# Thresholded attention with an FFN behind it: P left unscaled, 1/sum multiplied in at x, and some half tiles masked by GpSimd

## The chip, the core and the metric

The kernel runs on one core of a Trainium2 chip. The metric is the device time of one execution in microseconds (us). TensorE is called PE in the profile, VectorE DVE, ScalarE ACT, GpSimd POOL and SyncE SP.

## The reference

```
scores = q @ k^T / sqrt(64)                     # 8 batches, 8 heads, 576 rows, 64 columns
thresh = max(scores, -1) - tau                  # tau = 0.02
scores = where(scores >= thresh, scores, -1e9)
attn   = exp(scores - max(scores))
attn   = attn / (sum(attn, -1) + 1e-9)
x      = attn @ v                               # laid out as 4608 tokens x 512
h      = max(x @ w1, x @ w2, x @ w3)            # 512 x 768 each
out    = h @ w_out                              # 768 x 512
```

Of each row of 576 scores only those within tau of the row's maximum count. The rest gives zero.

## The kernel before

**Tiling.** A batch is cut into two quads of four heads. The four heads of a quad are two couples: r is 0 or 1, and i is the head within the couple. A quad has nine chunks, each of 128 rows of queries (chunk 4 holds the last 64 rows of two heads). A chunk has two half tiles, r = 0 and r = 1, each 128 x 576 scores. That makes 8 x 2 x 9 x 2 = 288 half tiles. q and k are loaded as rows and transposed on TensorE (`transposed`), and `swapped` copies qt to qs with the partition halves exchanged, so that two matmuls of 64 rows can run side by side.

**One half tile.** `scores` (line 324) writes sc, a PSUM bank. `maximum` (line 364) reads it on VectorE, writes z to SBUF and the row's maximum to nm. Then there are four kinds, given half tile by half tile by the digits of `MASKED`:

- kind 0: `threshold` makes th on VectorE, `exponents` runs a Prelu on ScalarE from z with the slope 2^-100 on one side, so that what is kept comes out tiny and what is masked does not, and `numerators` runs an Exp on ScalarE with scale -2^100 and its row sum
- kind 2 ("direct"): the same, with the Prelu reading the PSUM bank itself, which stays occupied until then
- kinds 1 and 3 (3 is direct): one Exp on ScalarE, then a `scalar_tensor_tensor` on VectorE that zeroes what lies below exp(-tau) and sums

All of them leave z in place. When both half tiles of a chunk are summed, `reciprocals` (line 396) makes rs on VectorE and `normalized` (line 400) makes P = z x rs in bf16, two instructions on GpSimd. `turned` (line 409) transposes P from SBUF to SBUF by a DMA on SP's queue, into ptq.

**From P to the output.** `product` (line 415) multiplies v by ptq into a PSUM tile o when all nine chunks of a quad are there. It is evacuated to xt in bf16: r = 0 by VectorE (`on_vector`), r = 1 by ScalarE (`on_scalar`). When both quads of a batch are in xt, `ffn` computes the three products ph with w1, w2 and w3 for six blocks of 128 (18 pieces, `hid`), takes their maximum (hm on ScalarE, then twice on VectorE, into hT) and multiplies with w_out (`outp`, `ninth`, `ninths_of_two`), evacuates po to ob and stores it. The last batch is split into two parts of its rows, chunks 0 and 1 and chunks 2 to 4 (`SPLIT`), which makes 18 parts of quads in all.

**Pools.** PSUM has four slots of two banks, chosen by the digit behind S, T, O, F and N in `ORDER`. z has nine buffers and, after the first 72, also the two of stage, through which the weights are loaded. P has six buffers.

**Order.** Every engine issues in program order, and SP's and ScalarE's DMAs are in that order too (`_Ordered` adds the ordering; all instructions issue at line 93, so that the profile shows L93 for nearly all of them). The order is the string `ORDER`, one letter an action. The letters that matter here: S scores, m maximum, s threshold, e the first pass, n the Exp of kinds 0 and 2, k the mask of kinds 1 and 3, r reciprocals, p one half of the normalization, t the DMA transpose, O product, x and w the evacuation of x by ScalarE and VectorE, F an FFN piece (18 hidden ones a part, then the outputs), v and h the evacuations of ph, u that of po, l loads, g and z loads and casts of weights, q and y the copies of q and v on GpSimd.

Of the kernel before, what the change touches and what calls it, by code (L numbers as in the profile page):

```python
# [11 lines left out]
F32 = mybir.dt.float32  # L12
# [3 lines left out]
OP = AluOpType  # L16
# [5 lines left out]
FLAT = 2.0 ** -100  # L22

MASKED = """
232222322322222222021032222202332122123122200200111000000000100000000011
000010111020011000101000000001100001001000010011111100000000100100000000
110010030111000100010000000001010100001110001011010100110000000000000000
100101101011000000120000001010000000110011100000001110001000010011111021
# [6 lines left out]
MORE_Z = 72  # L35
# [5 lines left out]
llllllglllT0laclT1laclzllqqS0qqS1meS2mS3lmlT0enlkS1ylmlT2eamelrnpS3leqlmnyS1qcapS0emtnrcS3pmnT2qmepgrelS1qya  # L41
gS0pmelT2mqnS3tcpemqS2nlkT1eytaS0rmnT1kpermS3yS2enczrmS1qT0enmepnqtS3nprmaymgpeS0lptS2mppT0mtpS1enencnqsS3re
rmtpS0mS1penmS3lqnsS2mtperpekzllmT0tmpenkT1pgS3eearnS0petmnqrS2meqlnpS3lmnplsS2cetpremS1pS0nmplermtzeS3mnS2p
mtnpmS3rkpS1leektS0emnrpmemptS1eekS2pO3mktS0rennmpermT2pnS1wptemS3prkyO0tmeakS2pgS1enxlnrmS0lpesS2mezT3mS1np
mgntspcS2eqrseT3mtpeS0srmapS1mnT2ptS3mnqO0ceqmeO1prswnptnkS3pxS0meF1meS2zBresmT0qghF3klpF2nkBtaS1sveS0pemF3B
nyrrsmyBepT1svS0hpcT2nS3zmaS1erpgsF2mntpsBmnS3yvF1etssT0myeBprS2cnpS3mnS0ympelF2epF3lmBnzslssvS0htBrqmeS2vpn
S1gF0sepmF3teqBmF2erssvpBtnBkphF0eS1vtS3znmF2nrBmqteS1rpvBnS3pmlnF0pmgeS1qsBsrhmS3pevS2npS1mF0npsO3ermpesmO2
zewepgsskBxtT3nF1vS2nklBarS0mlphS3mtepF2sS1rmnyBmetF3pvT0eBpcnS2tzT1nvS0asmzS3temS2qeS1meF0trkpmS3lenpBmnlys
reklpF1umerpskS3upBeoketmS0uS2umpS3tesmS1qeT0myO2nqlrsnlprcO3etqsmepwS0xptS1mnF3psnmS2BlerskpS1thF0meF3pmeBF
2ktnBveBsrS1nvpS0hmyF3emF2npBrssT0eprtvBaF1kS3nqvBeF0myhyS2kyleF3mBelBvnpS2snsS0vptemS1pnF3rmpT2tnBmpeF0scS1  # L50
htBrnmpF3erT2rpvlBasS1pstvnS2pmeF0pS3emtBqnmT2S1hcqS3empF2eS0rsqmtS1epsmBeF3pmnF0stsvBeBknF2klhF1BvelS0nrvpB
emT3pS2arvS0ptnS3mpnO1smtesrkpeF2swnlrpmeT0S1qtescS3epBmnpmnT0trskS3paS1umS0ulqmeS3lmyS1nopS2smelS0rmeS3psmn
O1ypersmqO2etkpemO0lewqxlknpS3tS1keF2momS3lexF0ktT1enkBercpnsBpumN1ertkphkF3jS0rursS1empBnmF2ptS0vpS1smeF3yt
BsnsmBpnvS0pT1hmF2atT3srepS0cF1eprBsmeqF3vnByBynvplS2nsS0plmhS1mteS2mF0nF3mteS1rrspBnmS2pelvBlepF1smT0leqBvl
aS2rkhF3oqnsS0mtS1epmBeqsF2ssmtS0epvBeyF1mnF3vpBesrS0ktphBermS1npT2svO0nytmpncT3eS1wF2nrmS0aBrsmnqF3vnT1pS0c
eBptsF2mhpS1eS3pmteS0qmBeO1spmnkteF3rvnpT0BsskapS2xvS0erS1qmtnS3pmnF2mqlespmeS1rtkBepresmT3puS1cuS0ptmnS3pS2
meyS1lrekpF0tnsmempO3lekteskO2nrsmpeBkpxrnwS1uptS3muS2pnmF0yoeS1mF3lesymBtnS2srkpS1hmBeF0spveF2ertBmpT3nrsvS
1paBlmpnS0tS3qhmF1epsmS2leBymF3tevF0nBknlS1rsvpS2esmqnBF3srmhpS1epS0tmeF2pssBrempBtesvS0ynF1mT3lnpBvF0lhsrcS
2tnT1mBnF3valS2nrBsqmeF0pvS1epS2meBptsmS3eqF1hmT2peBcS3tnskT2O0arkplnmO2lerpvewptS3xkpS1nF2meF0sstreBsmpS3nv
pBnmS1tS2hmT3eF0rmpnF1cBpnBrevptT3S2apvS0qmtS3S1enmqF2esrsqmiepmleS0soykeS1plBnmemtS3ukS0uT1snrlO2cpekynO1me  # L60
# [44 lines left out]
def kernel(  # L105
# [44 lines left out]
    def weight_loads():  # L150


        def piece(dst, src):
            my = {}

            def load():
                my["t"] = stage.tile([128, 4 * 256], F32, name="stage")
                sync.dma_start(out=my["t"].rearrange("p (k f) -> p k f", k=src.shape[1]), in_=src)
# [241 lines left out]
    def normalized(c):  # L400
        c["P"] = P = pp.tile([128, W], BF16, name="P")
        for n in range(2):
            pool.tensor_scalar(out=P[:, n * S:(n + 1) * S], in0=c["z", n],
                                    scalar1=c["rs"][:, n:n + 1], scalar2=1.0, op0=OP.mult, op1=OP.mult)
            if n:
                line["t"].append(c)
# [423 lines left out]
```

## Time and profile before

| | us |
|---|---|
| median of 3 runs | 447.64 |
| lowest and highest of them | 447.23 and 447.99 |
| span of the profiled execution, first to last instruction | 444.8 |
| median less that span | 2.8 |

The profiled execution is told by its span. A run's time also holds what lies ahead of the first instruction and behind the last, 2.8 us if the profiled execution was like the median. In the profile's groups a row gives line, engine, operation, output<-inputs, shapes and count, then the busy time and the mean duration of one in ns, then the engine's idle time ahead of them and what ended it. Durations of neighbours overlap, so the step from one start to the next is shorter than a duration. Rows of stretches of time give each engine's busy time, the granted clock of TensorE, the mean busy share of the DMA engines (it can be over 1, as packets overlap) and GB/s.

### The profile page before, as it was taken

The numbers are of one execution on the slowest core, as the hardware profiler recorded it, in microseconds if no ns is written. First come the engines' busy times: TensorE is split into PE (matmuls) and PEld (weight loads), VectorE is DVE, ScalarE is ACT, GpSimd is POOL, SyncE is SP. The second block draws the span as 40 slices with busy tenths as digits, with TensorE's granted clock in tenths as the row PEclk, the third lists the DMA queues.
The fourth block names the chain that finished last, engine by engine and source line by source line (L and its number), as shares of the span: only waits on it lengthen the run. The fifth ranks groups of instructions, "written<-read, shape, count | busy, mean of one in ns | idle before, by whom it ended". The sixth has DMA issues, their size and how long they took to land.

```text
span 444.8 us, 14254 instructions
## 1 busy us (share of the span) xinstructions
PE 422.4 (95%) x5188; PEld 320.2 (72%) x5190; DVE 392.8 (88%) x1228; ACT 403.0 (91%) x836; POOL 311.9 (70%) x420
## 2 busy tenths in 40 slices
PE   7767789999999999999999999999999999999996
PEld 6334347787788767787788777788688886787873
DVE  3887999999999999999999999998999998899642
ACT  3999999999999999999999999899999999987632
POOL 2799989997878687696785877676676685457400
PEclk8998999999999999999999999999999999999999
DMA  7999999999999999699899999989999977487633
GB/s 188 275 293 199 291 169 269 235 243 262 229 180 194 212 222 292 125 256 167 143 234 189 230 198 203 209 168 210 208 206 194 244 151 105 83 179 136 145 116 108
DMA packets 213959, 88.50 MB, mean 199 GB/s; under 512 B 189184, under 2 KB 202240, under 8 KB 213888
## 3 DMA queue, kind: packets, MB, share of 16 engines
q1 hardware_dynamic: 213360, 86.96, 95.9%
q8 instruction: 41, 0.67, 0.6%
q10 hardware_dynamic: 528, 0.62, 0.5%
q14 instruction: 30, 0.25, 0.2%
HBM read 35.65 MB, written 9.44 MB: 101 GB/s over the span
## 4 chain that ended last, share of the span: by engine, by line
PE 86%; ACT 5%; DVE 4%; issue 2%; DMA 1%; SPq 0%; DVEq 0%; ACTq 0%
PE ph L93 32%; PE sc L93 32%; PE po L93 10%; PE o L93 9%; ACT z L93 5%; PE tp L93 3%; DVE z L93 3%; DMA qm<-in_q_dram 1%; ACT qt L93 1%; SPq L93 0%; DVE xt L93 0%; DVE hm L93 0%; DVE stage L93 0%; DVE rs L93 0%; ACT ob L93 0%
## 5 line engine op out<-in xcount | busy, mean ns | idle before, releaser
L93 POOL TENSOR_SCALAR P<-z,rs 128x576 bf16<-128x576 f32 x250 | 200.6, 814 | 63.3 <-DVE rs L93 28.1
L93 DVE TENSOR_SCALAR_CACHE_REDUCE z<-sc 128x576 f32<-128x576 f32 x250 | 183.7, 750 | 14.8 <-PE sc L93 10.1
L93 PE MATMUL sc<-kt,qs 64*128 64x256 f32 (+2 forms) x640 | 182.6, 423 | 5.7 <-DVE z L93 2.3
L93 PE MATMUL sc<-kt,qt 64*128 64x320 f32 (+2 forms) x640 | 182.4, 433 | 5.2 <-ACT z L93 3.3
L93 PE MATMUL ph<-xt,w 64*128 64x288 bf16 (+2 forms) x2160 | 170.8, 283 | 0.1
L93 PEld LDWEIGHTS <-w 64*128 64x128 bf16 (+1 forms) x2160 | 130.1, 94 | 28.6 <-issue 4.3
L93 ACT ACTIVATE z<-z 128x576 f32<-128x576 f32 x174 | 117.6, 679 | 0.1
L93 PEld LDWEIGHTS sc<-kt,qs 64*128 64x128 f32 (+1 forms) x640 | 92.4, 180 | 25.7 <-DVE z L93 5.7
L93 ACT ACTIVATE z<-z,th 128x576 f32<-128x576 f32 x143 | 106.2, 769 | 5.0 <-DVE th L93 4.2
L93 PEld LDWEIGHTS sc<-kt,qt 64*128 64x128 f32 (+1 forms) x640 | 91.9, 179 | 19.7 <-ACT z L93 5.9
L93 DVE SCALAR_TENSOR_TENSOR z<-z 128x576 f32<-128x576 f32 x76 | 62.2, 830 | 0.5 <-ACT z L93 0.5
L93 PE MATMUL po<-wo,hT 64*128 64x512 bf16 (+3 forms) x454 | 53.5, 354 | 0.3
L93 POOL COPY qs<-qt 64x640 f32<-64x640 f32 (+3 forms) x66 | 43.0, 652 | 10.8 <-ACT qt L93 7.2
L93 ACT ACTIVATE z<-z,nm 128x576 f32<-128x576 f32 x68 | 50.6, 767 | 0.0
L93 DVE TENSOR_TENSOR hm<-ph,hm 128x576 bf16<-128x576 f32 (+2 forms) x54 | 37.0, 686 | 9.2 <-PE ph L93 8.9
L93 ACT ACTIVATE hm<-ph 128x576 bf16<-128x576 f32 (+2 forms) x54 | 31.8, 589 | 13.4 <-PE ph L93 12.8
L93 POOL TENSOR_SCALAR P<-stage,rs 128x576 bf16<-128x576 f32 x38 | 30.4, 804 | 19.3 <-ACT z L93 5.4
L93 PEld LDWEIGHTS <-hT 64*128 64x128 bf16 (+2 forms) x456 | 30.0, 95 | 16.5 <-issue 2.3
L93 DVE TENSOR_TENSOR hT<-ph,hm 128x576 bf16<-128x576 f32 (+2 forms) x54 | 37.0, 686 | 4.0 <-PE ph L93 2.3
L93 PE MATMUL o<-ptq,vb 128*64 128x64 bf16 (+2 forms) x544 | 39.0, 281 | 0.0
L93 ACT ACTIVATION_READ_ACCUMULATOR z<-z 128x1 f32 x174 | 34.3, 197 | 0.0
L93 PEld LDWEIGHTS <-vb 128*64 128x64 bf16 x544 | 23.3, 111 | 12.8 <-issue 4.9
(45 smaller groups left out, 431.6 us busy)
## 6 DMA issues: line engine op xcount, KB each, us to landing
vm<-in_v_dram SPq DMA_DIRECT2D x32, 256.0 KB, 4.8
qm<-in_q_dram SPq DMA_DIRECT2D x15, 512.0 KB, 5.0
km<-in_k_dram SPq DMA_DIRECT2D x15, 512.0 KB, 5.3
out_dram<-ob SPq DMA_DIRECT2D x14, 512.0 KB, 4.0
stage<-in_moe_w_dram SPq DMA_DIRECT2D x9, 512.0 KB, 5.2
ptq<-P SPq DMA_TRANSPOSE x144, 4.0
vr<-in_v_dram SPq DMA_DIRECT2D x16, 128.0 KB, 3.4
stage<-in_moe_w_out_dram SPq DMA_DIRECT2D x3, 512.0 KB, 4.9
```

Of the source, the lines that this page charges most:

```text
L93: ins = fn(*a, **kw)
```

## The change

P is left unscaled. `numerators` writes P itself, in bf16, each half into its place, and gives the row sum to a column of one tile per quad, `sm` (`sum_of`). `normalized` and `reciprocals` per chunk are gone, so that the transpose follows the second half's numerators.

For each part of a quad the new `reciprocals` takes 1/sum of all chunks on VectorE and transposes the 128 x 32 tile in blocks of 32 x 32. `scale_rows` (letter D) stores the result to DRAM, on SP's queue, and `scale_tile` (letter R) reads it back by two DMAs, each spread to 64 partitions, into R, a buffer of stage. The product's evacuation is one `tensor_tensor` on VectorE for both r = 0 and r = 1: xt = o x R.

39 half tiles become kind 4. `threshold` makes th = nm + tau, `set_apart` (letter b) runs two instructions on GpSimd, a `tensor_scalar` that writes 2^100 where z > th and 0 elsewhere, and a `tensor_tensor` that adds this to z. Then one Exp on ScalarE with its sum (letter X) writes P. The counts by kind (0, 1, 2, 3, 4) are 169, 78, 33, 8, 0 before and 141, 75, 22, 11, 39 after.

The half tiles of z no longer use stage, ob9 takes buffers of z, small tiles have 8 buffers and not 6, and `ORDER` and `MASKED` are new throughout.

```diff
 FLAT = 2.0 ** -100
+FAR = 2.0 ** 100
 MASKED = """
...
-    def half_of_z():
-        n = next(halves_of_z)
-        if n >= MORE_Z and (n - MORE_Z) % (ZBUFS + 2) >= ZBUFS:
-            return stage.tile([128, 4 * 256], F32, name="stage")[:, :S]
-        return zz.tile([128, S], F32, name="z")
+    def by_pool(c, r):
+        return by_mask[2 * number[c["g"], c["idx"]] + r] == "4"
...
     def threshold(c, r):
         th = c["th", r] = small.tile([128, 1], F32, name="th", bufs=5)
-        vector.tensor_scalar(out=th, in0=c["nm", r], scalar1=-1.0, scalar2=tau, op0=OP.mult, op1=OP.subtract)
+        if by_pool(c, r):
+            vector.tensor_scalar(out=th, in0=c["nm", r], scalar1=tau, scalar2=None, op0=OP.add)
+        else:
+            vector.tensor_scalar(out=th, in0=c["nm", r], scalar1=-1.0, scalar2=tau, op0=OP.mult, op1=OP.subtract)
+    def set_apart(c, r):
+        z, m = c["z", r], half_of_p(c, r)
+        pool.tensor_scalar(out=m, in0=z, scalar1=c["th", r], scalar2=FAR, op0=OP.is_gt, op1=OP.mult)
+        pool.tensor_tensor(out=z, in0=z, in1=m, op=OP.add)
...
     def numerators(c, r):
-        z, acc = c["z", r], c["sm"][:, r:r + 1]
-        if masked(c["g"], c["idx"], r):
-            vector.scalar_tensor_tensor(out=z, in0=z, scalar=thr, in1=z,
+        z, p, acc = c["z", r], half_of_p(c, r), sum_of(c, r)
+        if by_pool(c, r):
+            scalar.activation(out=p, in_=z, func=AF.Exp, bias=c["nm", r], scale=-1.0, accum_out=acc)
+        elif masked(c["g"], c["idx"], r):
+            vector.scalar_tensor_tensor(out=p, in0=z, scalar=thr, in1=z,
                                         op0=OP.is_ge, op1=OP.mult, accum_out=acc)
         else:
-            scalar.activation(out=z, in_=z, func=AF.Exp, scale=-1.0 / FLAT, accum_out=acc)
-    def reciprocals(c):
-        c["rs"] = small.tile([128, 2], F32, name="rs")
-        vector.reciprocal(c["rs"], c["sm"])
-    def normalized(c):
-        c["P"] = P = pp.tile([128, W], BF16, name="P")
-        for n in range(2):
-            pool.tensor_scalar(out=P[:, n * S:(n + 1) * S], in0=c["z", n],
-                                    scalar1=c["rs"][:, n:n + 1], scalar2=1.0, op0=OP.mult, op1=OP.mult)
+            scalar.activation(out=p, in_=z, func=AF.Exp, scale=-1.0 / FLAT, accum_out=acc)
...
+    def reciprocals(g, part, n):
+        L, t = Ls[g], turns[n % 2]
...
+            vector.reciprocal(new[:, :, f:f + 9], sums[:, :, f:f + 9])
...
+            vector.reciprocal(new[to, :, at:at + 1], sums[of, :, was:was + 1])
+        vector.transpose(t[:, 1, :], t[:, 0, :])
+    def scale_rows(g, part):
+        s["rows"] = rows.tile([32, 128], F32, name="rows")
+        sync.dma_start(out=s["rows"].rearrange("j (b t) -> b j t", b=4), in_=s["t"][:, 1, :])
+    def scale_tile(g, part):
+        s["R"] = stage.tile([128, W], F32, name="stage").rearrange("p (r n) -> p r n", r=2)[:, :, 0:n]
...
+        for i in range(2):
+            sync.dma_start(out=s["R"][64 * i:64 * i + 64],
+                           in_=src[i, :, o:o + n].unsqueeze(0).to_broadcast([64, 2, n]))
...
-        def on_vector():
-            vector.tensor_copy(out=dst[:, lo:hi], in_=ps[:, base:base + hi - lo])
-        def on_scalar():
-            scalar.activation(out=dst[:, lo:hi], in_=ps[:, base:base + hi - lo], func=AF.Copy)
+        def done():
+            vector.tensor_tensor(out=dst[:, lo:hi], in0=ps[:, base:base + hi - lo],
+                                 in1=scales[2 * L["b"] + L["qd"], part]["R"][:, r, :], op=OP.mult)
```

185 lines of the change are left out of this document (112 added, 73 removed).

## The prediction

> **What bounds the kernel now.** I read the page's head first, then busy time in three stretches, then the groups by shape, then the waits of the first stretch.
>
> ```profile
> span 444.8 us, 14254 instructions
> PE 422.4 (95%) x5188; PEld 320.2 (72%) x5190; DVE 392.8 (88%) x1228; ACT 403.0 (91%) x836; POOL 311.9 (70%) x420
> L93 PE MATMUL ph<-xt,w x2160: 272/283/299, 73.1 to 435.5; 64*128 64x288 bf16 x184, 128*128 128x320 bf16 x7, 128*128 128x256 bf16 x6
> core 0: us, PE busy (x) PEld busy (x) DVE busy (x) ACT busy (x) POOL busy (x), PEclk, DMA share, GB/s
> 0.00:73.00 73.00, 56.29 (x502) 33.94 (x503) 58.19 (x178) 63.96 (x138) 56.99 (x81) 0.93 1.07 239
> 73.00:412.00 339.00, 337.74 (x4407) 265.23 (x4405) 320.55 (x1021) 326.61 (x672) 250.10 (x334) 1.00 1.00 198
> 412.00:444.80 32.80, 28.38 (x284) 21.03 (x282) 14.11 (x33) 12.43 (x29) 4.77 (x7) 0.99 0.44 125
> ```
>
> The first FFN matmul (ph) starts at 73.1 us. Before it TensorE has only scores and products to do and stands idle for 73.00 - 56.29 = 16.7 us. ScalarE is the busiest there (63.96), VectorE has 58.19 and GpSimd 56.99. So the opening runs at the pace of **ScalarE**. From 73 to 412 us TensorE is busy 337.74 of 339.00 us: the middle is **TensorE's**, with ScalarE at 96% and VectorE at 95% close behind. The last 33 us are one chain of TensorE and evacuations.
>
> ```profile
> 126.33 2.94 PE ph L93 x48
> 195.04 1.96 PE ph L93 x32
> PEld sc L93 <- ACT z L93: 10.0, 19, 1.0
> PEld sc L93 <- DVE z L93: 5.9, 7, 1.8
> ```
>
> In the chain of waits an FFN matmul costs 2.94 / 48 = 0.061 us, and 1.96 / 32 = 0.061 us elsewhere: where TensorE has work it goes at one rate, and nothing a vector engine gives back makes it faster. The two waits are those of the opening (0 to 73 us): score matmuls that stand until ScalarE (10.0 us) or VectorE (5.9 us) has freed a PSUM bank. So a gain must come from the opening, from the 1.3 us of idle TensorE in the middle, or from the end.
>
> **The change part by part.** I take the steps of the engines from rows that stand back to back, since one instruction's end overlaps the next one's start.
>
> ```profile
> 99.31 0.68 ACT L93 ACTIVATE z<-z 128x576 f32<-128x576 f32 x1
> 99.89 0.20 ACT L93 ACTIVATION_READ_ACCUMULATOR z<-z 128x1 f32 x1
> 99.98 1.44 ACT L93 ACTIVATE z<-z,th 128x576 f32<-128x576 f32 x2
> 100.22 0.76 DVE L93 TENSOR_SCALAR_CACHE_REDUCE z<-sc 128x576 f32<-128x576 f32 x1
> 100.91 0.15 DVE L93 TENSOR_SCALAR th<-nm 128x1 f32<-128x1 f32 x1
> 100.97 0.75 DVE L93 TENSOR_SCALAR_CACHE_REDUCE z<-sc 128x576 f32<-128x576 f32 x1
> L93 ACT ACTIVATE z<-sc,nm 128x576 f32<-128x576 f32 x39 | 28.3, 746 | 2.9 <-DVE z L93 2.9
> L93 DVE SCALAR_TENSOR_TENSOR z<-z 128x576 f32<-128x576 f32 x76 | 62.2, 830 | 0.5 <-ACT z L93 0.5
> L93 DVE RECIPROCAL rs<-sm 128x2 f32<-128x2 f32 x144 | 22.0, 157 | 2.0 <-ACT z L93 1.4 <-ACT stage L93 0.2
> L93 DVE CAST xt<-o 128x576 bf16<-128x576 f32 x14 | 10.5, 749 | 0.5 <-PE o L93 0.5
> L93 ACT ACTIVATE xt<-o 128x576 bf16<-128x576 f32 x14 | 9.0, 640 | 0.2
> L93 DVE TENSOR_TENSOR hm<-ph,hm 128x576 bf16<-128x576 f32 x42 | 31.5, 751 | 0.8 <-PE ph L93 0.6
> L93 POOL TENSOR_SCALAR P<-z,rs 128x576 bf16<-128x576 f32 x250 | 200.6, 814 | 63.3 <-DVE rs L93 28.1 <-ACT z L93 11.6 <-DVE th L93 7.4
> 0.00:73.00 73.00, 36.58 (x46) 0.93 1.07 239
> ```
>
> Steps: ScalarE's Exp with its sum 99.98 - 99.31 = 0.67 us; a Prelu from z 1.44 - 0.77 = 0.67; a Prelu straight from PSUM about 0.64 (its 746 ns less the same overlap of 0.1). VectorE's maximum 0.69, its threshold 0.06, a masking multiply 0.75 (830 ns less 0.08). The last row counts GpSimd's instructions on P alone (its one number of busy time): 36.58 us in the opening.
>
> *ScalarE in the opening.* The order issues, ahead of its first FFN piece, 50 first passes and 37 Exps before (37 of those passes direct from PSUM), and 34 first passes, 23 Exps and 12 masked Exps after, 10 of the passes direct. Before: 37 x 0.64 + 13 x 0.67 + 37 x 0.67 = 57.2. After: 10 x 0.64 + 24 x 0.67 + 35 x 0.67 = 45.9. The two x evacuations that leave ScalarE there are 2 x 0.53 = 1.1 more. Together 12.4 us less: 64.0 becomes 51.6.
>
> *VectorE in the opening.* One more maximum (+0.7), 31 thresholds for 8 (+1.4), 11 masking multiplies for 12 (-0.75), 4 x evacuations for 2 (+1.3), 23 small reciprocals gone (0.08 each in step, -1.8), and for two units the new reciprocals with a 32x32 transpose. That transpose has no row; between the small reciprocal (0.16) and the 749 ns cast I take 0.2, the small one, as it streams 32 columns. That is 0.36 a unit, +0.7. Sum +1.6: 58.2 becomes 59.8. **VectorE takes over as the busiest.** The multiply by R reads a second f32 operand from SBUF; its bounds are the 751 ns of hm and the masking multiply's 830; I take 751.
>
> *GpSimd.* Its 36.6 us on P go. 12 half tiles come, each a tensor_scalar of one input (0.81) and an add of two inputs, which no row shows: between 0.81 and twice that, 1.6, for two inputs read one after the other. I take 1.6, so 12 x 2.4 = 28.8 and 57.0 becomes 49.2, below VectorE at either end. The Trainium skill (GPSIMD Engine Reference, § 4.1 Engine selection and § 3.1) says that two-input elementwise work belongs on VectorE, GpSimd being about half as fast at 2.6 cycles an element; by that an estimate of 576 x 2.6 / 1.2 GHz = 1.25 us for the add, and the sum stays.
>
> So the opening's busiest engine falls from 64.0 to 59.8 us: **-4.2**. Half tiles that hold a PSUM bank until ScalarE has read it fall from 37 to 10 of some 54, so of the 10.0 us of waits above most go; what matters of them is the idle time they pass on, and I add **-1.3**. Bounds for the opening: 0 (it is not ScalarE's pace) and -12.4 (VectorE is no bound).
>
> *The middle.* ScalarE loses work, VectorE keeps its sum (144 small reciprocals fewer, 36 of the new ones, 18 transposes and 18 evacuations more). TensorE can only give back its idle **-1.3**; the bounds are -6 and +4, a percent or two of 339 for another order of the pieces.
>
> *The way through DRAM.* For each of 18 parts one store of 16 KB and two loads of 64 partitions x 2 x 576 x 4 B = 295 KB (fewer in the last batch), 9.4 MB beside 88.5 MB.
>
> ```profile
> DMA packets 213959, 88.50 MB, mean 199 GB/s; under 512 B 189184, under 2 KB 202240, under 8 KB 213888
> vm<-in_v_dram SPq DMA_DIRECT2D x32, 256.0 KB, 4.8
> k<-in_k_dram SPq DMA_DIRECT2D x7, 128.0 KB, 3.3
> out_dram<-ob SPq DMA_DIRECT2D x3, 64.0 KB, 2.6
> 136.50 1.40 SPq L93 DMA_DIRECT2D vr<-in_v_dram  x2
> SPq L93 <- POOL P L93: 130.9, 83, 6.0
> ```
>
> Store 2.6, an issue 0.7, then the second load 4.8 x 295 / 256 = 5.5: a trip of 8.8 us from the transpose to a complete R. In the compiled order I counted VectorE's work between each transpose and the first multiply that needs it: 7.1 us in the twelfth part, 8.6 in the second and fourth, 9.3 in the fourteenth, over 10 in the other middle ones. So the twelfth is late by 1.7, two by 0.2: 2.1 us, of which the banks ahead of TensorE cover some: **+1.0**. SP gets 54 DMAs more, at 0.7 us 38 us; each second one waits for the store with transposes queued behind. Against that its 130.9 us of waits for GpSimd's P go, as a transpose now follows the Exp. If that cover fails, each trip holds the transposes 2.6 us. By the fixed 2 us per DMA of the Trainium skill (DMA: Bandwidth & Descriptors, Anatomy of one DMA) with its 436 GB/s, an estimate of 2.0 + 2.0 + 1.4 = 5.4 us for the trip; then the +1.0 drops out. The rows above have each DMA dearer than that.
>
> *The end.*
>
> ```profile
> 417.55 0.42 DVE L93 TENSOR_TENSOR hm<-ph,hm 128x256 bf16<-128x256 f32 x1 [0.29 <-PE ph L93]
> 423.99 0.49 DVE L93 CAST xt<-o 128x320 bf16<-128x320 f32 x1 [0.24 <-PE o L93]
> 424.69 0.44 ACT L93 ACTIVATE xt<-o 128x320 bf16<-128x320 f32 x1 [2.02 <-PE o L93]
> 425.88 1.39 PE L93 MATMUL ph<-xt,w 128*128 128x320 bf16 x9
> ```
>
> The last reciprocals now stand behind the second hm of these (417.55 + 0.42), so they and the transpose are done near 418.5. Store 2.6, issue 0.7, and a load of 164 KB, between 3.3 and 4.8, say 3.7: R is whole at 425.5, and the two multiplies, now one after the other on VectorE, end at 426.4. The FFN matmuls that need x started at 425.88: **+0.5**.
>
> Sum: -4.2 - 1.3 - 1.3 + 1.0 + 0.5 = -5.3. The span goes from 444.8 to 439.5. The three runs had a median of 447.64, 2.8 above the span, so **442.3 us**.
>
> **The rivals.**
>
> *R lands late and VectorE stands.* VectorE takes its instructions in order, so a multiply whose R has not landed holds the maxima behind it, and with them the PSUM banks and TensorE. Place: the second, fourth, twelfth and fourteenth parts and the end. Against it: the 8.8 us trip above. For it: DMA share 1.07 and 1.00 in the first two stretches, to which 10.6% of bytes are added. A trip of 12 us is late by 3.4 + 3.4 + 4.9 + 2.7 = 14.4, by some 3 in the parts at 10.7 to 11.6, and by 3 more at the end. VectorE is 95% busy and cannot win it back: 442.3 - 1.0 + 20 = 461. It decides from about 10 us, where 6.4 us in the middle and 1.2 at the end are lost and the gain is gone.
>
> *GpSimd's two passes come late.* ScalarE's Exp then stands in its queue for a masked z. At 1.6 us for the add the chain from threshold to Exp is 2.4 us; contention can stretch it, as it does P's 814 ns mean. One us late in each of 39 is 39 us on an engine that has 5 to 10% to spare; a quarter of that on the path gives 452. It decides from some 0.15 us of lateness each. It is the one that the skill's rule above speaks for. It would show as ScalarE waiting for GpSimd.
>
> *The opening is not ScalarE's.* DMA at share 1.07, the loads and the in-order waits between engines set 73 us as well. Then only -1.3 + 1.0 + 0.5 is left: about 447.8, no change.
>
> *The new order feeds TensorE better.* With ScalarE at 90% and not 96% in the middle and banks free earlier, some of the 6 us of the bound come: 436.
>
> **How the numbers follow.** Forecast 0.52, better fed 0.17, opening unchanged 0.08, R late 0.15, GpSimd late 0.08. A measurement here can tell about 0.2%, 0.9 us, from no change. Faster by more: the first two, 0.69. Within: 0.05 of the unchanged opening. Slower: its other 0.03 and the two late ones, 0.26. The forecast with its bounds goes from 436 to 446. The range takes in most of the better fed case down to 433 and GpSimd late up to 453; left out are the dear end of R late and the tail of the fourth, under 0.2.
>
> **What would show it.** Right: first ph near 67.5 us and not 73.1; VectorE, not ScalarE, busiest ahead of it; waits of score weights for ScalarE well under 10 us; no VectorE wait for the R tile's DMA over 2 us; from the first ph to the last scores about 338 us. Wrong: a first ph at 72 or later, VectorE waits on the load from DRAM in several parts, ScalarE waits for GpSimd, a GpSimd add over 2 us, or a TensorE that is idle over 1% in the middle.

## The result and the profile after

The changed kernel takes **521.41 us** (median of 4 runs, 515.81 to 524.21), the kernel before, run beside it, 447.81 us. The ratio is 1.161, 95% interval 1.154 to 1.167: 73.6 us slower, where 5.3 us faster was forecast. The ratio leaves out the run of 524.21 us, which was in a slower state of the machine. The profiled execution, 515.81 us, is the fastest of the four, so that its span shows 513.7 - 444.8 = 68.9 us of the loss.

From the page of the changed kernel: its head, the FFN matmuls by tile (count, shortest, median and longest in ns, first and last start), and the busy time in the prediction's first two stretches.

```profile
span 513.7 us, 13809 instructions
PE 453.1 (88%) x5188; PEld 307.9 (60%) x5190; DVE 411.4 (80%) x1169; ACT 383.5 (75%) x779; POOL 226.3 (44%) x210
L89 PE MATMUL ph<-xt,w x2160: 269/283/444, 80.8 to 504.4; 64*128 64x288 bf16 x184, 128*128 128x320 bf16 x7, 128*128 128x256 bf16 x6
0.00:73.00 73.00, 54.48 (x464) 34.84 (x466) 53.95 (x174) 50.12 (x106) 59.67 (x55) 0.86 0.98 214
73.00:412.00 339.00, 306.62 (x3706) 208.74 (x3701) 287.62 (x804) 275.93 (x560) 146.92 (x139) 0.97 1.00 207
```

Three things are to be seen. The opening did not get shorter: the first FFN matmul starts at 80.8 us (before: 73.1), and the busiest engine ahead of it is now GpSimd (59.67 us of 73). The middle has lost its bound: between 73 and 412 us no engine is busy for more than 306.62 of 339 us, where TensorE was at 337.74 before. And the end is as it was: from the last FFN matmul's start to the end of the span are 513.7 - 504.4 = 9.3 us, as before (444.8 - 435.5). So the loss lies in the opening (7.7 us) and above all between first and last FFN matmul: 423.6 us against 362.4, that is 61.2 us.

TensorE's granted clock fell as well, from 0.988 over the span before to 0.957, and to 0.59 between 40 and 60 us, where TensorE is busy for 12.59 of 20 us. No run separates what the clock itself adds to the loss.

A kernel in which every engine idles is waiting in turns. The chain of waits says on whom, by engine and by tile:

```profile
PE 44%; POOL 17%; DMA 12%; ACT 9%; DVE 9%; issue 8%; SPq 0%; POOLq 0%; DVEq 0%; ACTq 0%
PE ph L89 23%; PE sc L89 12%; POOL P L89 11%; DMA ptq<-P 7%; POOL z L89 5%; DVE z L89 4%; ACT z L89 4%; ACT P L89 4%; PE po L89 3%; DMA stage<-rows 3%; PE o L89 3%; PE tp L89 2%; DMA rows<-turn 2%; DVE P L89 1%; ACT hm L89 1%
```

In the profile before, the first of these lines was

```profile
PE 86%; ACT 5%; DVE 4%; issue 2%; DMA 1%; SPq 0%; DVEq 0%; ACTq 0%
```

TensorE had 86% of the chain and has 44%. New on it are GpSimd's two passes (P 11%, z 5%), the transposes of P (7%, where all DMA had 1%) and the trip of the reciprocals (stage<-rows 3%, rows<-turn 2%). The groups price GpSimd's passes, and the waits (total us, times, longest) say who stands for them:

```profile
L89 POOL TENSOR_SCALAR P<-z,th 128x576 bf16<-128x576 f32 x39 | 89.6, 2297 | 86.7 <-DVE th L89 53.0
L89 POOL TENSOR_TENSOR z<-z,P 128x576 f32<-128x576 f32 x39 | 51.5, 1320 | 3.3
ACT P L89 <- POOL z L89: 56.0, 32, 4.2
...
DVE xt L89 <- DMA stage<-rows: 6.5, 4, 2.6
```

A half tile costs GpSimd 2.30 + 1.32 = 3.6 us, where the prediction had 2.4, and ScalarE waits for 32 of the 39, 56.0 us in all. VectorE's waits for R, the last row, come to 6.5 us. In the timeline one such wait is seen whole (start, duration, engine, instruction, and in brackets the idle time before it):

```profile
33.77 2.21 POOL L89 TENSOR_SCALAR P<-z,th 128x576 bf16<-128x576 f32 x1 [0.37 <-DVE th L89]
36.06 1.28 POOL L89 TENSOR_TENSOR z<-z,P 128x576 f32<-128x576 f32 x1
```

```profile
34.21 0.76 ACT L89 ACTIVATE z<-z,nm 128x576 f32<-128x576 f32 x1
37.37 0.78 ACT L89 ACTIVATE P<-z,nm 128x576 bf16<-128x576 f32 x1 [2.40 <-POOL z L89]
```

ScalarE has done its first pass over another half tile at 34.97 us and its next instruction in program order is the Exp of this half tile. It stands for 2.40 us, and all that is queued behind that Exp with it.

### The profile page after: what moved, and what is told of

Read it like the earlier page. It is cut to its first block, busy times and chain, and to the rows that moved or that the text cites. A ratio compares the mean times of both kernels' runs of the same rounds, so it can differ in the third digit from the quotient of the medians.

```text
span 513.7 us, 13809 instructions
## 1 busy us (share of the span) xinstructions
PE 453.1 (88%) x5188; PEld 307.9 (60%) x5190; DVE 411.4 (80%) x1169; ACT 383.5 (75%) x779; POOL 226.3 (44%) x210
## 4 chain that ended last, share of the span: by engine, by line
PE 44%; POOL 17%; DMA 12%; ACT 9%; DVE 9%; issue 8%; SPq 0%; POOLq 0%; DVEq 0%; ACTq 0%
PE ph L89 23%; PE sc L89 12%; POOL P L89 11%; DMA ptq<-P 7%; POOL z L89 5%; DVE z L89 4%; ACT z L89 4%; ACT P L89 4%; PE po L89 3%; DMA stage<-rows 3%; PE o L89 3%; PE tp L89 2%; DMA rows<-turn 2%; DVE P L89 1%; ACT hm L89 1%
## 5 line engine op out<-in xcount | busy, mean ns | idle before, releaser
L89 DVE TENSOR_SCALAR_CACHE_REDUCE z<-sc 128x576 f32<-128x576 f32 x288 | 208.9, 750 | 22.4 <-PE sc L89 19.7
L89 PE MATMUL ph<-xt,w 64*128 64x288 bf16 (+2 forms) x2160 | 181.2, 291 | 12.2 <-ACT hm L89 5.2
L89 PEld LDWEIGHTS <-w 64*128 64x128 bf16 (+1 forms) x2160 | 113.4, 97 | 71.5 <-PE ph L89 34.6
L89 POOL TENSOR_SCALAR P<-z,th 128x576 bf16<-128x576 f32 x39 | 89.6, 2297 | 86.7 <-DVE th L89 53.0
L89 ACT ACTIVATE P<-z 128x576 bf16<-128x576 f32 x163 | 109.8, 674 | 5.7 <-DMA ptq<-P 4.0
L89 DVE SCALAR_TENSOR_TENSOR P<-z 128x576 bf16<-128x576 f32 x86 | 73.5, 864 | 21.1 <-ACT z L89 16.8
L89 ACT ACTIVATE P<-z,nm 128x576 bf16<-128x576 f32 x39 | 30.2, 774 | 56.3 <-POOL z L89 56.0
L89 POOL TENSOR_TENSOR z<-z,P 128x576 f32<-128x576 f32 x39 | 51.5, 1320 | 3.3
L89 PE MATMUL o<-ptq,vb 128*64 128x512 bf16 (+2 forms) x544 | 39.6, 285 | 1.8 <-DVE z L89 1.4
L89 PEld LDWEIGHTS <-hT 64*128 64x128 bf16 (+2 forms) x456 | 25.3, 95 | 24.6 <-issue 4.5
L89 POOL CAST vb<-vm 128x1024 bf16<-128x1024 f32 x16 | 17.4, 1089 | 40.4 <-issue 26.7
```

Of the source, the lines that this page charges most:

```text
L89: ins = fn(*a, **kw)
```

## The experiments

Three theories stood ahead of the first runs. **A**: GpSimd's slow pass, through ScalarE's in-order queue, is the loss. **B**: it is the new order of TensorE's pieces. An FFN piece of the first seven batches has two halves of 64 partitions which swap their places, and the second (letter B) first waits, by a semaphore, for the end of the first one's last matmul (letter F). Counted in the two strings, a B is the very next TensorE piece behind its own F once in 140 before and 96 times in 140 after. The prediction gave this no price. **C**: it is the trip of the reciprocals through DRAM. Each run is compared with the kernel before in the same set of runs (medians 446.8 to 447.9 us).

**quick_mask.** GpSimd's first pass gets two operations that run fast there and multiply by zero, so the mask of the 39 half tiles is left out.

```diff
-        pool.tensor_scalar(out=m, in0=z, scalar1=c["th", r], scalar2=FAR, op0=OP.is_gt, op1=OP.mult)
+        pool.tensor_scalar(out=m, in0=z, scalar1=c["th", r], scalar2=0.0, op0=OP.mult, op1=OP.mult)
```

> The changed kernel, but in GpSimd's first pass of the 39 half tiles the compare (is_gt, mult) is two multiplies (mult, mult by 0). It leaves out the mask in those 39 half tiles. Theory A, the compare is what makes that pass take 2.30 us and ScalarE stand 56 us for z: the pass falls to about 0.8 us, ScalarE's waits for GpSimd's z to under 10 us, and the time from 521 to 470 to 490 us. Theory B, TensorE's gates behind their own first halves carry the loss: the waits at the gates (34.6 us) stay, and the time stays over 510. Theory C, the trip through DRAM carries it: over 510 as well.

Measured: 501.45 us, ratio 1.123 (1.118 to 1.127). The pass and ScalarE's waits:

```profile
L89 POOL TENSOR_SCALAR P<-z,th 128x576 bf16<-128x576 f32 x39 | 35.7, 915 | 108.2 <-DVE th L89 79.6 <-issue 11.4 <-DMA ptq<-P 9.2
ACT P L89 <- POOL z L89: 19.9, 16, 4.3
```

The waits fall by 36 us and the loss against before by 19. A is right as a mechanism and too small as the cause: 54.6 us of loss are left. The time lies between the 470 to 490 of theory A and the 510 of the others, and none of the three holds alone.

**apart.** The changed kernel with 61 of the 96 adjoining second halves moved behind the next TensorE piece of the order, which leaves 21 directly behind their first half.

```diff
-O1wS2qllygwS0nnmlmF1eBF3skeesnte
...
+O1wS2qllygwS0nnmlmF1eF3Bskeesnte
...
```

> The changed kernel, but in 61 of the 96 places where the second half of a matmul piece is issued directly behind its own first half, the next TensorE piece is put between the two. Nothing else moves. Theory B: the waits of weight loads for ph fall from 34.6 us to about 13, and the time falls by 15 to 25 us, to 497 to 507. Theory A: GpSimd sets the pace, what TensorE no longer waits at its gates it waits at its banks, and the time stays within 5 us of 521.

Measured: 523.89 us, ratio 1.171 (1.166 to 1.176), no gain. **glued** is the other side of it: the kernel before with every B put directly behind its F.

```diff
-mgntspcS2eqrseT3mtpeS0srmapS1mnT2ptS3mnqO0ceqmeO1prswnptnkS3pxS0meF1meS2zBresmT0qghF3klpF2nkBta
...
+mgntspcS2eqrseT3mtpeS0srmapS1mnT2ptS3mnqO0ceqmeO1prswnptnkS3pxS0meF1BmeS2zresmT0qghF3BklpF2Bnkta
...
```

> The kernel before, with each second half of a matmul piece moved up to stand directly behind its first half, 139 places of 140 and not 1. Theory B: each gate waits some 0.38 us for the last matmul of its first half, 40 to 53 us in all, and the time rises to 485 to 500. Rival: the gate's wait is hidden by the matmuls still running, and the time stays within 5 us of 448.

Measured: 495.40 us, ratio 1.109 (1.106 to 1.112). The weight loads' wait for their own piece, in glued, after and apart:

```profile
PEld L93 <- PE ph L93: 46.5, 126, 0.4
```

```profile
PEld L89 <- PE ph L89: 34.6, 90, 0.6
```

```profile
PEld L89 <- PE ph L89: 7.7, 21, 0.4
```

A hidden second half behind its own first half waits 46.5 / 126 = 0.37 us. In glued the 139 that were moved there come to the whole loss of 48.5 us (0.35 each), in a kernel that TensorE bounds. In apart 26.9 us of the same wait go and the time stays: TensorE does not bound the changed kernel, so what it saves at a gate it waits for elsewhere. Theory B falls as the cause, and the same wait is worth its full price in one kernel and nothing in the other. **quick_apart** (both edits) says the same.

> Both of these edits at once; it leaves out the mask in 39 half tiles. If A and B are both real and add up, the time is 445 to 465 us. If only A is, it is that of the run with the quick mask. If the trip through DRAM costs much (theory C), it stays over 475.

Measured: 503.86 us, ratio 1.126 (1.120 to 1.131), as quick_mask alone.

**no_trip** and **trip_by_gpsimd** start from quick_apart (so no mask in 39 half tiles). no_trip leaves the store and the loads of R out and copies x unscaled; trip_by_gpsimd issues them from GpSimd's queue.

```diff
-        sync.dma_start(out=s["rows"].rearrange("j (b t) -> b j t", b=4), in_=s["t"][:, 1, :])
...
-            vector.tensor_tensor(out=dst[:, lo:hi], in0=ps[:, base:base + hi - lo],
-                                 in1=scales[2 * L["b"] + L["qd"], part]["R"][:, r, :], op=OP.mult)
+            vector.tensor_copy(out=dst[:, lo:hi], in_=ps[:, base:base + hi - lo])
```

> The run with the quick mask and the pieces apart, less the way through DRAM: 1/sum and its transpose are still made, but not stored or read back, and x is evacuated by a plain copy on VectorE. It leaves out the mask in 39 half tiles and the scaling by 1/sum. Theory C, R's two loads stand at the head of SP's queue until the store has landed and a stage buffer is free of weights, with the transposes of P behind them: VectorE and ScalarE no longer wait for transposes to free P, and the time falls from 504 to 450 to 470 us. Theory D, the new order itself does not fit the engines: the time stays over 490.

Measured: 487.66 us, ratio 1.088 (1.083 to 1.094), between the two theories: the trip costs 16 us here.

```diff
-        sync.dma_start(out=s["rows"].rearrange("j (b t) -> b j t", b=4), in_=s["t"][:, 1, :])
+        pool.dma_start(out=s["rows"].rearrange("j (b t) -> b j t", b=4), in_=s["t"][:, 1, :])
...
-            sync.dma_start(out=s["R"][64 * i:64 * i + 64],
+            pool.dma_start(out=s["R"][64 * i:64 * i + 64],
```

> The run with the quick mask and the pieces apart, with the store of the sums and the two loads of R issued by GpSimd and not by SP; bytes, buffers and waits are the same. It leaves out the mask in 39 half tiles. Theory C in the form that what hurts is the place in SP's queue: 465 to 485 us. If it is the bytes or the shared stage buffer: within 8 us of 504.

Measured: 523.30 us, ratio 1.170 (1.162 to 1.177), 19 us slower than by SP, which neither answer foresaw.

```profile
POOL rows L89 <- DVE turn L89: 57.4, 10, 12.8
ACT P L89 <- POOL z L89: 30.6, 17, 5.8
DVE xt L89 <- DMA stage<-rows: 27.1, 7, 9.4
```

GpSimd stands 57.4 us with a store that waits for VectorE's transpose, and the mask passes queued behind it are late for ScalarE. GpSimd's queue is no way out here, as it has in-order work that others wait for.

**mask_by_scalar.** The changed kernel with the 39 half tiles masked by ScalarE: at the letters b and X it does the Prelu and the Exp of kind 0. Nothing is left out.

```diff
-        pool.tensor_scalar(out=m, in0=z, scalar1=c["th", r], scalar2=FAR, op0=OP.is_gt, op1=OP.mult)
-        pool.tensor_tensor(out=z, in0=z, in1=m, op=OP.add)
+        scalar.activation(out=z, in_=z, func=AF.Prelu, bias=c["th", r], scale=1.0, alpha=FLAT)
...
-            scalar.activation(out=p, in_=z, func=AF.Exp, bias=c["nm", r], scale=-1.0, accum_out=acc)
+            scalar.activation(out=p, in_=z, func=AF.Exp, scale=-1.0 / FLAT, accum_out=acc)
```

> The changed kernel with its 39 half tiles masked by ScalarE's Prelu in place of GpSimd's two passes, at the same places of the order; nothing is left out. ScalarE gets 39 x 0.67 = 26 us more work. Theory A: GpSimd's chain of 3.6 us is gone, and the time is that of the quick mask, 495 to 505 us, or below. If GpSimd's pass were innocent: 521 or more.

Measured: 493.40 us, ratio 1.102 (1.097 to 1.107). ScalarE gets 39 passes more and the kernel is 28 us faster. **GpSimd's masks cost 28 us**, net of these passes.

**forms.** A small kernel that only times GpSimd instructions on 128 x 576, with nothing beside them; it computes none of the reference.

```diff
+    for name, dt, a, b, s2 in forms:
+        t = one.tile([128, 576], dt, name=name)
+        for _ in range(4):
...
+                nc.gpsimd.tensor_scalar(out=t, in0=z, scalar1=th, scalar2=s2, op0=a, op1=b)
```

> Not the kernel: four instructions each on GpSimd alone, 128x576, f32 in, with a scalar from SBUF: is_gt and mult, mult and mult, subtract and mult, subtract and max, is_ge and mult, max and mult, is_gt alone, to bf16, the first two also to f32, and tensor_tensor add, subtract and mult. The output is zeros. Theory A: the forms with a compare take 2.2 us, the arithmetic ones about 0.75, whatever the type of the output. Rival: every form is fast here, and the 2.3 us in the kernel come from VectorE or the DMA beside it.

Its groups (the tile's name tells the operations: gtmul is is_gt then mult, mulmul is mult then mult, maxmul max then mult, gtonly is_gt alone, ttadd and ttaddb the add with a second operand in f32 and in bf16):

```profile
L111 POOL TENSOR_SCALAR gtmul<-z,th 128x576 bf16<-128x576 f32 x4 | 8.8, 2211 | 3.3 <-DMA z<-in_moe_w_dram 3.1
L111 POOL TENSOR_SCALAR maxmul<-z,th 128x576 bf16<-128x576 f32 x4 | 8.8, 2211 | 0.3
L109 POOL TENSOR_SCALAR gtonly<-z,th 128x576 bf16<-128x576 f32 x4 | 6.9, 1730 | 0.0
L115 POOL TENSOR_TENSOR ttadd<-z,y 128x576 f32<-128x576 f32 x4 | 5.6, 1394 | 0.0
L120 POOL TENSOR_TENSOR ttaddb<-z,mm 128x576 f32<-128x576 f32 x4 | 5.1, 1272 | 0.0
L111 POOL TENSOR_SCALAR mulmul<-z,th 128x576 bf16<-128x576 f32 x4 | 3.0, 746 | 0.3
```

With no other compute engine at work the pass takes 2211 ns, 96% of its 2297 in the kernel: it is not contention. Nor is it the comparison, as theory A had it: max with mult takes the same. What is special is mult with mult, the one form that the profile before showed.

**scalar_no_trip**: mask_by_scalar with the trip left out, x copied unscaled.

> The changed kernel's own order, with ScalarE in GpSimd's place at the 39 half tiles (as mask_by_scalar) and without the trip (x is copied unscaled, so that x is computed without the reciprocals of the sums): what is left of the change is its order. Theory D: 470 to 485 (mask_by_scalar's 493 less 8 to 20 for the trip), 25 to 35 us above before. Theory F (slow passes and trip were the whole of it, and each hid the other): 448 to 460.

Measured: 473.45 us, ratio 1.058 (1.053 to 1.063). **The trip costs 20 us** here (493.40 to 473.45).

**old_order_full** and **old_order_no_trip** put the same code into the order and mask kinds of before (theory D: what is left is the new order).

```diff
-042122100122401004144103442234102040104404010010000000001110000100101000
+232222322322222222021032222202332122132123122200200111000000000100000000011
...
-lllllT2laqcT1acqqqS0msS3lS1emmnlllesS2T3lS0bamT2nlqlcS3S1qlaqmqeclS2emmXS1nllmmylS0S2glS1esmmtT3sekneatkmyqy
+llllllglllT0laclT1laclzllqqS0qqS1meS2mS3lmlT0enlkS1ylmlT2eamelntS3leqlmnyS1qcaS0emncS3tmnT2qmegelS1qyagS0tme
+lT2mqnS3cemqS2nlkT1eyaS0mnT1ktemS3yS2enczmS1qT0enmenqS3ntmaymgeS0ltS2mtT0mS1enencnrDqsS3emtS0mS1enmS3lqnsS2m
...
```

> The idea in the order of before: the code of the changed kernel (P unscaled, the reciprocals by way of DRAM, x multiplied by R at VectorE) with the mask kinds and the order of before; no half tile is masked by GpSimd. The letters of the 288 scalings of P and the 144 reciprocals are gone, each transpose of P is issued where the first scaling of its P stood, all 36 evacuations of x are VectorE's, the 18 sets of reciprocals and stores stand behind the last numerators of their unit and the loads of R 14 letters or more behind those. 76 first halves of hidden rows and their second halves stand as in before. Theory D (what is left of the loss is the new order, which does not fit the engines): 445 to 465, that is the trip's late loads and no more. Theory E (the idea itself costs it, by P buffers that are held from the numerators to the transpose and by x at VectorE alone): 475 to 500.

> As old_order_full, without the trip: the stores and loads of R are left out and x is copied unscaled, so that x is computed without the reciprocals of the sums. Theory D: 438 to 450, at or below before, since the 312 us of GpSimd's scalings are gone and nothing has come for them but 18 copies of x. Theory E: 470 to 490, as far from before as no_trip was (488).

Measured: 486.88 us, ratio 1.088 (1.080 to 1.095), and 472.94 us, ratio 1.057 (1.050 to 1.063). The second is what scalar_no_trip takes, 25 us above before in either order. The 473.45 of scalar_no_trip lay in theory D's range too, but with the old order the loss stays, so theory D falls and the numbers of theory E hold. On balance the order is worth 0.5 us, less than these runs can tell. (The 312 us in old_order_no_trip's expectation are all that GpSimd was busy before; the scalings are 200.6 us of it for 250 half tiles and 30.4 for the other 38.) The order is a balance, as the FFN matmuls of scalar_no_trip and old_order_no_trip show:

```profile
L89 PE MATMUL ph<-xt,w x2160: 269/283/299, 70.3 to 461.9; 64*128 64x288 bf16 x184, 128*128 128x320 bf16 x7, 128*128 128x256 bf16 x6
```

```profile
L89 PE MATMUL ph<-xt,w x2160: 269/283/444, 77.8 to 461.4; 64*128 64x288 bf16 x184, 128*128 128x320 bf16 x7, 128*128 128x256 bf16 x6
```

The new order starts them 7.5 us earlier and takes 391.6 us for them, against 383.6. The waits of second halves behind their own first ones are 33.3 us in the first of these kernels and 0.4 in the second; whether moving them apart would pay there was not tried.

What a trip is made of is seen in old_order_full's second one, ahead of that kernel's first FFN matmul (85.8 us), first in VectorE's timeline, then in SP's:

```profile
64.34 0.21 DVE L89 STREAM_TRANSPOSE turn<-turn 128x32 f32<-128x32 f32 x1
...
83.64 0.76 DVE L89 TENSOR_TENSOR xt<-o,stage 128x576 bf16<-128x576 f32 x1 [5.41 <-DMA stage<-rows]
```

```profile
65.58 1.34 SPq L89 DMA_TRANSPOSE ptq<-P  x1
67.02 0.61 SPq L89 DMA_DIRECT2D rows<-turn  x1
67.72 4.82 SPq L89 DMA_TRANSPOSE ptq<-P  x3
72.64 0.54 SPq L89 DMA_DIRECT2D stage<-in_moe_w_dram  x1
73.23 0.51 SPq L89 DMA_DIRECT2D km<-in_k_dram  x1
73.80 0.67 SPq L89 DMA_DIRECT2D vm<-in_v_dram  x1
74.58 1.25 SPq L89 DMA_DIRECT2D stage<-rows  x2
```

The transpose on VectorE is done at 64.55, the store issues 2.5 us later, behind a transpose of P, and the loads 7.6 us after the store, behind three more transposes (1.6 us of SP's queue each) and three loads; R has landed 8 us behind them. The whole takes 19.1 us, and VectorE stands 5.41 us.

**unscaled_alone** asks which part of the idea makes the 25 us. Order and masks of before; the numerators write P, and scalings, reciprocals and trip are left out, x on both engines as before. It does less work than the kernel before, but has the buffers of the changed kernel: nine of z, the ninth rows' output among them, and one tile of sums for a quad. The diff is against the changed kernel; the order and the masks are new besides.

```diff
-        sync.dma_start(out=s["rows"].rearrange("j (b t) -> b j t", b=4), in_=s["t"][:, 1, :])
...
-            vector.tensor_tensor(out=dst[:, lo:hi], in0=ps[:, base:base + hi - lo],
-                                 in1=scales[2 * L["b"] + L["qd"], part]["R"][:, r, :], op=OP.mult)
+            src = ps[:, base:base + hi - lo]
+            if r == 0:
+                vector.tensor_copy(out=dst[:, lo:hi], in_=src)
+            else:
+                scalar.activation(out=dst[:, lo:hi], in_=src, func=AF.Copy)
```

> One part of the change alone, in the order and with the masks of before: the numerators write P as bf16 themselves, and the 288 scalings by GpSimd and the 144 reciprocals are left out, with nothing in their place (no trip, no scaling of x, so x is computed without the reciprocals of the sums). x is copied by VectorE and ScalarE in turn, as before. Theory G (a buffer of P is now taken at the first half's numerators, which ScalarE and VectorE write, and held until the transpose has read it; with six of them the two busiest engines now wait where GpSimd did): 460 to 475, most of the 25 us of old_order_no_trip. Theory H (those 25 us are the reciprocals set behind the last numerators and x at VectorE alone): 440 to 450.

Measured: 458.85 us, ratio 1.029 (1.025 to 1.033): 12 us slower than before with less work, 14 us better than old_order_no_trip. Neither theory as it stood, and the run does not test P's buffers alone, since the other buffers differ from before's. **unscaled_five_p**, **unscaled_seven_p** and **before_five_p** change the number of P's buffers (unscaled_alone, five_p and seven_p had eight, six and five of each small tile, so that the first two comparisons hold a second difference). The diff is before_five_p's.

```diff
-PBUFS = 6
+PBUFS = 5
```

> unscaled_alone with five buffers of P instead of six (it leaves out the same). Theory G: slower than unscaled_alone by 10 to 30 us. Theory H: within 5 us of it.

> unscaled_alone with seven buffers of P instead of six; to make room the weights' staging tiles are back at 1024 columns, and there are five small tiles of a kind instead of six and four thresholds instead of five (it leaves out the same). Theory G: faster than unscaled_alone by 5 to 20 us. Theory H: within 5 us of it, unless the fewer small tiles cost it some.

> The kernel before with five buffers of P instead of six, nothing else. Theory G: P is taken only when GpSimd writes it, so that a buffer fewer costs little here, 0 to 6 us, less than in unscaled_five_p against unscaled_alone. Theory H: no matter, 0 to 3.

Measured: 461.62 us, ratio 1.033 (1.029 to 1.036); 456.47 us, 1.022 (1.019 to 1.024); 448.65 us, 1.004 (1.002 to 1.006). ScalarE's wait for a buffer of P with six (unscaled_alone) and with seven:

```profile
ACT P L89 <- DMA ptq<-P: 7.7, 6, 3.4
DVE P L89 <- DMA ptq<-P: 7.5, 5, 3.3
```

```profile
ACT P L89 <- DMA ptq<-P: 0.4, 1, 0.4
```

The wait is real (15.2 us on the two engines, none in the profile before), and a buffer more takes it away, but only 2.4 us of time. Five instead of six cost 2.8 us here and 1.9 in the kernel before: theory G's contrast was not there, and theory H's small numbers hold in all three.

**unscaled_late_t** puts the transposes at their old letters, and **no_trip_late** adds to it the reciprocals 14 letters behind the last numerators and all x on VectorE (the diff is no_trip_late's order against old_order_no_trip's).

```diff
-llllllglllT0laclT1laclzllqqS0qqS1meS2mS3lmlT0enlkS1ylmlT2eamelntS3leqlmnyS1qcaS0emncS3tmnT2qmegelS1qyagS0tme
-lT2mqnS3cemqS2nlkT1eyaS0mnT1ktemS3yS2enczmS1qT0enmenqS3ntmaymgeS0ltS2mtT0mS1enencnrDqsS3emtS0mS1enmS3lqnsS2m
...
+llllllglllT0laclT1laclzllqqS0qqS1meS2mS3lmlT0enlkS1ylmlT2eamelnS3leqlmnyS1qcaS0emtncS3mnT2qmegelS1qyagS0melT
+2mqnS3tcemqS2nlkT1eytaS0mnT1kemS3yS2enczmS1qT0enmenqtS3nmaymgeS0ltS2mT0mtS1enencnqsS3emtS0mS1enmS3lrDRqnsS2m
...
```

> unscaled_alone with each transpose of P at its own old letter, some letters later than the first scaling of its P stood (it leaves out the same: no reciprocals, x unscaled). In unscaled_alone the delay against before, matmul by matmul, came in steps (6.8 us between 176 and 187 us), where SP stood at transposes whose numerators were not done, or issued six transposes in a row and the buffers of P came back late. Theory I (the place of the transposes in SP's queue, since SP issues in order and one transpose takes it 1.8 us): 445 to 453. Theory G (the buffers of P, which are held still longer so): 460 to 468.

> old_order_no_trip with each transpose of P at its own old letter, and the reciprocals 14 letters behind the last numerators of their unit and not directly behind them (it leaves out the loads and stores of R, and x is unscaled). Against unscaled_late_t it adds 54 small instructions of VectorE (11 us) and 18 copies of x that were ScalarE's (12 us). Theory H' (the wait of the reciprocals for ScalarE was what old_order_no_trip lost over unscaled_alone): within 4 us of unscaled_late_t. Rival (VectorE's 23 us more of work): 8 to 14 us above it.

Measured: 462.66 us, ratio 1.033 (1.026 to 1.040), and 467.84 us, 1.044 (1.039 to 1.049). Theory I falls: the transposes' place is not it (the later one came out 3 us slower, within the intervals). Of the 10 us by which old_order_no_trip lies above unscaled_late_t, 5 go with the later place of the reciprocals and the transposes and 5 stay for VectorE's added work; both answers held in part. In unscaled_late_t the longest single wait of TensorE, VectorE and ScalarE was a new one:

```profile
DVE z L89 <- DMA out_dram<-z: 5.5, 1, 5.5
```

A half tile's z waits for a store: the change gave the ninth rows' output a buffer of z, of which there are nine now for eleven.

**before_unscaled** therefore takes the kernel before with its own buffers, and only the numerators write P (scalings and reciprocals left out).

```diff
-            scalar.activation(out=z, in_=z, func=AF.Exp, scale=-1.0 / FLAT, accum_out=acc)
+            scalar.activation(out=p, in_=z, func=AF.Exp, scale=-1.0 / FLAT, accum_out=acc)
```

> The kernel before itself, with its eleven buffers of z, its own buffer for the outputs of the ninth rows and its sums per block of rows; the one edit is that the numerators write P as bf16, and that the scalings of P and the reciprocals are left out (x is computed without the reciprocals of the sums). Each transpose stands at its own old letter. Theory J (the 15 us of unscaled_late_t are the smaller things that the change did beside it: nine buffers of z for eleven, the ninth rows' outputs in a buffer of z, one tile of sums for a whole quad): 444 to 450. Theory G (the buffers of P, held from the first numerators): 455 to 465, with waits of the two engines for buffers of P of 8 us or more, as in unscaled_late_t.

Measured: 451.69 us, ratio 1.009 (1.005 to 1.012): between the two theories, nearer to J's 450 than to G's 455. Ten of the 15 us of unscaled_late_t were the smaller edits (fewer buffers of z, the ninth rows in them, one tile of sums for a quad); they were not told apart from each other. The remaining 4.7 us come of the one edit, the numerators' writing P. Theory G's sign, waits for a buffer of P of 8 us or more, is there:

```profile
ACT P L89 <- DMA ptq<-P: 6.6, 8, 1.4
DVE P L89 <- DMA ptq<-P: 6.4, 3, 4.2
```

That these 13.0 us of waits are what costs the 4.7 is not shown: in unscaled_seven_p 14.8 us of such waits went for 2.4 us of time.

**The sum.** Taking the change back step by step, each kernel against the kernel before of its own set:

| from, to | us above before | the step |
|---|---|---|
| the change | 73.6 | |
| mask_by_scalar | 45.5 | GpSimd's masks, 28.1 |
| scalar_no_trip | 25.8 | the trip through DRAM, 19.7 |
| old_order_no_trip | 25.3 | order and mask kinds, 0.5 |
| no_trip_late | 20.3 | reciprocals (and transposes) later, 5.0 |
| unscaled_late_t | 15.1 | VectorE's reciprocals and x, 5.2 |
| before_unscaled | 4.7 | buffers of z, ninth rows, sums, 10.4 |
| before | 0 | P written by the numerators, 4.7 |

By the intervals of the ratios a step is good to 3 to 4 us, the last to 1.5: 0.5 is nothing, and 5.0 and 5.2 are just clear of it. Each belongs to its place in this sequence: the trip was worth 16 us in no_trip and 13.9 in the old order (486.88 - 472.94). In scalar_no_trip TensorE's granted clock is 0.988 as before, so the last 25 us are not the clock's.

## Why the prediction was wrong

- **"each a tensor_scalar of one input (0.81)"** is the step that failed first. The price was taken from `P<-z,rs`, which is mult with mult; the new one is is_gt with mult and takes 2.30 us in the kernel, 2.21 by itself. The step named bounds for the add only and none for this operation, as if it had a row. The add, bounded at 0.81 and 1.6, took 1.32. The rival "GpSimd's two passes come late" was the true mechanism of this part, with ScalarE waiting for GpSimd as it said. Its 452 was mis-sized: it had 1 us of lateness for each of 39 half tiles and 10 us of time; ScalarE stood 56.0 us in 32 of them, and they cost 28.1. The Trainium skill (GPSIMD Engine Reference, § 4.1 Engine selection) says that two-input elementwise work is slow on GpSimd and one-input work roughly at line rate. The trace agrees for mult with mult (746 ns for 576 columns) and contradicts it for every other pair tried (2211 to 2215 ns), so that here the one-input pass was the dearer of the two.
- **The opening, -4.2 and -1.3.** It failed through the same price and through the trip. GpSimd's 12 half tiles were to take 28.8 us of it there. Its instructions on P alone, from 0 to 73 us:

```profile
0.00:73.00 73.00, 42.35 (x24) 0.86 0.98 214
```

  These 42.35 us for two instructions each of 12 half tiles made it the busiest engine. The larger part is the trip's: the first FFN matmul starts at 80.8 us in the changed kernel, at 77.7 with the masks on ScalarE and at 70.3 without the trip as well, so that 3.1 us are the masks' and 7.4 the trip's, which the sum had late by 0.2 us in the opening. The 70.3 are 2.8 us better than before where 5.5 were forecast, but in a kernel in which ScalarE does these masks, so they do not show the forecast's own mechanism.
- **The middle, -1.3 with bounds -6 and +4.** This is the largest miss: 61.2 us between the first and the last FFN matmul. "Nothing a vector engine gives back makes it faster" is right; its converse was left out. With ScalarE at 96% and VectorE at 95% of that stretch, their waits can reach TensorE, and TensorE at 99.6% cannot win them back: its idle time from 73 to 412 us went from 1.3 to 32.4 us. Bounds by "another order of the pieces" did not hold that case, and the order was worth nothing on balance. The constant 0.061 us of an FFN matmul was also read from places where no B follows its F; 0.37 us a piece stood behind that (34.6 us in the changed kernel), without a price there, as apart shows, because TensorE was no longer the bound.
- **The trip, +1.0.** The legs were right where SP's queue is short: in the last part VectorE's transpose is done at 487.13 and the first multiply starts at 493.52, 6.4 us where 7.0 were forecast.

```profile
486.92 0.21 DVE L89 STREAM_TRANSPOSE turn<-turn 128x32 f32<-128x32 f32 x1
...
493.52 0.89 DVE L89 TENSOR_TENSOR xt<-o,stage 128x320 bf16<-128x320 f32 x2 [0.87 <-DMA stage<-rows]
```

  Between the legs the sum had no queue. Elsewhere SP's transposes and loads stand between store and loads, as in the 19.1 us above; the second part's trip, 8.8 us in the sum, takes 12.9 in the changed kernel (66.39 to 79.30). And the cover "its 130.9 us of waits for GpSimd's P go" did not come true, as SP now waits for ScalarE and the reciprocals instead:

```profile
SPq L89 <- ACT z L89: 74.1, 48, 3.6
SPq L89 <- ACT P L89: 53.2, 33, 5.5
SPq L89 <- DVE turn L89: 21.1, 6, 5.3
```

  So the rival "R lands late and VectorE stands" held. It shows best in mask_by_scalar, where GpSimd's masks are out of the way:

```profile
PE sc L89 <- DVE xt L89: 13.3, 5, 4.8
...
DVE xt L89 <- DMA stage<-rows: 12.2, 4, 5.1
...
PEld sc L89 <- DVE xt L89: 8.0, 4, 3.7
```

  VectorE stands for R, and score matmuls and weight loads (in part at the same moments) for VectorE's evacuation of x; without the trip, in scalar_no_trip, only 1.4 us of the last row are left. In the changed kernel the three are 7.9, 6.5 and 7.1 us. The rival's price, some 20 us, is near the 14 to 20 measured, in part by luck: in the changed kernel VectorE stood in the second, tenth and twelfth parts and at the end, and the rival had named the second, fourth, twelfth and fourteenth and the end.
- **Not priced at all**: P written by the numerators, its buffers held from then to the transpose (4.7 us in all), nine buffers of z for eleven and the ninth rows' output among them (10.4 us with the sums' tile), the reciprocals directly behind the last numerators (5.0 us with the transposes' places, which moved in the same run).
- **Right**: the multiply by R (749 ns, forecast 751), the end (the last part's first FFN matmul starts 8.2 us behind the hm ahead of the reciprocals, 7.9 before: +0.3 where +0.5 was forecast), and VectorE's work as a sum (its groups come to 473.6 us, 469.8 before), though the step that gave it the new reciprocals and all of x cost 5.2 us.

## What to carry to other kernels

A row prices an operation only for the operations in it: a tensor_scalar with another pair of ALU operations is an operation without a row, and gets bounds or a measurement of its own. Where three in-order engines are nearly full, as here in the middle (99.6, 96 and 95%), a new hand-over between two of them can cost far more than its instructions, but waits have no one price: 36 us less of ScalarE's waits for GpSimd gave 19 us, 14.8 us less of waits for P's buffers gave 2.4. Ask of each moved write which buffer it now holds, and for how long, and measure it. A DMA's duration is not a trip's duration: count what stands in the issuing queue between its legs (6.4 us with a short queue, 12.9 and 19.1 with other DMAs between).

## What the runs showed of the hardware

- GpSimd's tensor_scalar on 128 x 576 f32 takes 746 ns for mult with mult and 2.21 us for is_gt, is_ge, max or subtract with a second operation; is_gt alone takes 1730 ns. For is_gt with mult, output in f32 or bf16 makes no difference (2213 and 2211).
- Its tensor_tensor takes 1394 ns for an add of two f32 operands and 1272 with one of them in bf16.
- In glued a weight load that waits by a semaphore for the end of the matmuls issued directly before it stands 0.37 us on average (46.5 us, 126 times).
- Less work can take longer: before_unscaled drops the scalings (200.6 us of GpSimd in the row of the prediction alone) and the reciprocals, adds nothing, and is 0.5 to 1.2% slower than the kernel before.
